# Cluster-masked attention and two MoE layers on one core: the first pair's cluster steps split by head, waits and priorities of the attention's planner set anew

## The chip, the core and the metric

The kernel runs on one core of a Trainium2 chip. A core has a matrix engine (PE, TensorE; its weight loads are listed as PEld), a vector engine (DVE, VectorE), a scalar engine (ACT, ScalarE), a general engine (POOL, GpSimd), and SP (SyncE), which issues the transfers. The metric is the device time of one execution in microseconds. A difference of less than 0.2% (1.2 us) is about what a measurement of this kernel cannot tell from no change.

## The reference

Two batches of eight heads, 768 tokens of 64 elements each, attend within clusters; the result goes through two layers.

```python
q_assign = np.argmax(np.einsum('bhsd,hcd->bhsc', q_n, c_n), axis=-1)
k_assign = np.argmax(np.einsum('bhsd,hcd->bhsc', k_n, c_n), axis=-1)
mask = q_assign[:, :, :, None] == k_assign[:, :, None, :]
scores = np.where(mask, scale * np.matmul(q, k.transpose(0, 1, 3, 2)), -1000000000.0)
scores = scores - np.max(scores, axis=-1, keepdims=True)
attn = np.exp(scores)
attn = attn / (np.sum(attn, axis=-1, keepdims=True) + 1e-09)
x = matmul(attn, v)                  # 1536 tokens x 512
h = x @ w_in                         # 512 x 2048
x = (h * sigmoid(1.702 * h)) @ w_out
# then a second layer: x @ w2_in, a softmax-weighted product, a norm, @ w2_out
```

There are 16 clusters; `q_n`, `k_n` and `c_n` are rows divided by their norms.

## The kernel before

**The attention.** There are 16 units u, one for each head and batch, taken in eight pairs p of two heads. For each pair the queries and keys are loaded (`load`), transposed on PE (`turn`, L557) into `ex`, split into a high and a low part (`turn_high` on ACT, `turn_low` L573 on DVE), and multiplied with the centroids. The products are copied and turned again, and then the cluster steps on DVE find each token's cluster: the maximum (`cluster_max`, L608), equality with it (L614), a weighting that picks the first of equals (L617), a maximum again (L623), and two comparisons that write the one-hot code `oh` (`cluster_halves`, L631, two instructions of half the size). The code of the first pair is turned on PE by `cluster_rows` (L647) and put in place by `cluster_place` (L655); `cluster_turn` (L639) turns the whole of it, and moves (L664, issued by SP) bring the rest into `OP`, the operands of the scores.

For each unit there are nine score tiles m of 512 columns, in two passes. The first pass, `sm` (`peak`, L936), computes scores with the clusters' codes appended; DVE takes the negative maximum of each token (`nma`, `peak_max`, L947), a small reduction makes `nm` of it (L959), PE turns that (L963), and it goes into the operands, for the first four units by `peak_rows` (L968) and for the others by a copy (L980) and a move. The second pass, `st` (`score`, L995 and L996), computes the scores less their maximum; ACT takes the exponential (L1004), ACT or DVE casts it to 16 bits (`cast`, L1009), POOL or DVE computes what the cast left off (`rest`, L1013), and PE multiplies both with the values (`av`, L1028, L1031, L1032). A further part on DVE and ACT normalizes the result (L1043 to L1058).

The values are scaled by powers of two that are worked out on DVE from 128x1 columns: `powers`, `factor` (L821, one product of two such columns) and `x_power` (L852 and L853, two products). POOL computes the low part of the values (`values_low`, L795 and L796).

**The layers.** `hps` (L1200) is the first product of the first layer; its weights are prepared on DVE during the attention (L196, L201, L205). The layers follow an order of their own, which starts where the attention's ends.

**What sets the order.** Every step is entered by `add` with the cost on each engine that may do it, a due time, the steps that it comes after, and the PSUM buffer that it takes or frees. `Plan.order` then simulates the engines: at each turn it takes, of the steps that are possible now, the one with the earliest due time, and the instructions are emitted in that order. Each engine works its own list strictly in order. A step marked `shared` on DVE is not placed beside a POOL step. SHIFTS is a table that adds to the due times of single steps, by their number. With STAY above zero, PE prefers for a while to stay with one kind of matmul. What a step waits for on the chip is set by the data that it touches, not by the planner's list.

Of the kernel before, what the change touches and what calls it, by code (L numbers as in the profile page):

```python
# [9 lines left out]
F32 = mybir.dt.float32  # L10
# [11 lines left out]
def kernel(  # L22
# [22 lines left out]
    P = 128  # L45
# [28 lines left out]
    XDUE = 30  # L74
    VDUE = 15
    VLC = dict(DVE=0.93, POOL=2.55)
    SOON = 10
# [18 lines left out]
    STAY = 0.0  # L96
# [71 lines left out]
    class Weight:  # L168
# [434 lines left out]
    def groups(t):  # L603
        return t.rearrange("p (g o) -> p g o", o=1).to_broadcast([P, G, C])

    def cluster_max(t, p):
        mxs[p] = oh_p.tile([P, G], F32, tag="mx", name="mx")
        nc.vector.tensor_reduce(out=mxs[p], in_=t["tile"], op=ALU.max, axis=AX.X)  # L608

    def cluster_equal(t, p):  # L610


        eqs[p] = t["tile"]
        nc.vector.tensor_tensor(out=eqs[p], in0=t["tile"], in1=groups(mxs[p]), op=ALU.is_equal)  # L614

    def cluster_weigh(p):
        nc.vector.tensor_tensor(  # L617
            out=eqs[p], in0=eqs[p], in1=first.rearrange("p (o c) -> p o c", o=1).to_broadcast([P, G, C]), op=ALU.mult
        )

    def cluster_first(p):
        m2s[p] = oh_p.tile([P, G], F32, tag="m2", name="m2")
        nc.vector.tensor_reduce(out=m2s[p], in_=eqs[p], op=ALU.max, axis=AX.X)  # L623

    def cluster_halves(p):

        eq = eqs.pop(p).rearrange("p (j s i) c -> p s j i c", s=2, i=2)
        m2 = m2s.pop(p).rearrange("p (j s i o) -> p s j i o", s=2, i=2, o=1)
        ohs[p] = oh_p.tile([P, NJ, 2, 2, C], BF16, tag="oh", name="oh")
        for s, op in enumerate((ALU.is_lt, ALU.is_equal)):  # L630
            nc.vector.tensor_tensor(  # L631
                out=ohs[p][:, :, s], in0=eq[:, s], in1=m2[:, s].to_broadcast([P, NJ, 2, C]), op=op
            )
# [54 lines left out]

    def operands_of(p):
# [4 lines left out]
        for s in range(2):  # L694
# [7 lines left out]
            for i in range(2):  # L702
                T["L", p, s, i] = add(
                    dict(SP=(0.65, 1.0)), n0 + LDUE if p > 1 else -62, lambda t, s=s, i=i: load(p, s, i),
                    after=[at("TT", p - 1, 2)] + late(True) if p > 1 else [],
                )
        for e in range(3):
# [4 lines left out]
                after=[a, at("ST", 2 * (p - NHL) + 1, NU - 1)],  # L712
# [5 lines left out]
        for n in range(2):  # L718
# [10 lines left out]
        b = add(dict(DVE=0.47), n0 + 18, lambda t, a=a: cluster_max(a, p), after=[a, at("C4", p - 1)])  # L729
        b = add(dict(DVE=0.47), n0 + 18, lambda t, a=a: cluster_equal(a, p), after=[b])  # L730
        b = add(dict(DVE=0.47), n0 + 19, lambda t: cluster_weigh(p), after=[b])
        b = add(dict(DVE=0.47), n0 + 20, lambda t: cluster_first(p), after=[b])
        b = T["C4", p] = add(
            dict(DVE=0.54), n0 + 21, lambda t: cluster_halves(p), after=[b, at("TO", p - 1)], frees=a
        )
        for e in range(0 if p else 3):
            a = add(dict(PE=0.3), n0 + 21, lambda t, e=e: cluster_rows(t, e), after=[b], take="ex")
# [4 lines left out]
        a = T["TO", p] = add(dict(PE=0.45), n0 + 22, lambda t: cluster_turn(t, p), after=[b], take="ex")  # L742
# [4 lines left out]
        for i in range(2):  # L747
            u = 2 * (p - NS) + i
            before = [at("ST", u, NU - 1), at("SM", u, NU - 1)]
# [58 lines left out]
    def values():  # L808
# [50 lines left out]
        add(dict(DVE=1.1), XDUE, lambda t, a=a: x_power(a), after=[a, scales["v"]], frees=a)  # L859
        T["VF"] = add(dict(DVE=0.1), 8, lambda t: factor(), after=list(scales.values()))  # L860
# [211 lines left out]
    def peaks_of(u):  # L1072
# [21 lines left out]
        if u >= RWS:  # L1094
# [9 lines left out]
            T["RW", u] = add(dict(SP=(0.65, 0.05)), n0 + NU - 18, lambda t: peak_row(u), after=[a, at("ST", u - 4, NU - 1)])  # L1104
# [3 lines left out]
    def scores_of(u):  # L1108
# [45 lines left out]
        if i:  # L1154
            a = add(
                dict(ACT=0.73, DVE=0.5), n + 12, lambda t: x_high(t, p), after=[T["N", u], T["N", u - 1], at("TX", p - 1, 0)],
# [150 lines left out]
    for p in range(NH // 2):  # L1307
# [743 lines left out]
```

## Time and profile before

| | |
|---|---|
| median of 3 runs | 592.21 us (592.07 to 593.05) |
| profiled execution | 592.09 us |
| its span in the trace | 590.3 us |
| PE busy | 579.9 us (98%) |
| DVE, ACT, POOL busy | 454.1, 418.5, 278.7 us |
| granted PE clock | 1.00 in every window |
| first matmul of hps | 219.65 us |

The span runs from the first to the last instruction that the trace holds; the execution's own time is 1.8 us longer. "Busy" of PE includes matmuls that overlap in its pipeline, so a busy PE can still be a little late.

### The profile page before, as it was taken

What the parts mean: (1) busy time and instruction counts of PE and PEld (TensorE: products, weight loads), DVE (VectorE), ACT (ScalarE), POOL (GpSimd) and SP (SyncE); (2) the same over time, 40 slices, a digit from 0 to 9 for tenths busy, and PEclk for the clock granted to TensorE, in tenths of its full rate; (3) what the DMA queues carried; (4) which work ended last, traced back from release to release, by engine and by line L of the source; (5) the groups of instructions that cost most, each with busy time, mean ns of one, the idle gap of its engine ahead of it and who ended that gap; (6) DMA issues with size and microseconds to landing.
All of it is one profiled execution on the core that took longest, in us unless ns stands there. A gap on an engine that the chain in (4) does not pass through costs nothing.

```text
span 590.3 us, 12602 instructions
## 1 busy us (share of the span) xinstructions
PE 579.9 (98%) x4790; PEld 387.1 (66%) x4790; DVE 454.1 (77%) x924; ACT 418.5 (71%) x799; POOL 278.7 (47%) x262
## 2 busy tenths in 40 slices
PE   7999999999999999999999999999999999999997
PEld 5788888888888876666666666666655664444444
DVE  5999998898999997899888731984996427996820
ACT  5799989988999978788878356563647614647831
POOL 7469979977778764344682037802100300133100
PEclk9999999999999999999999999999999999999999
DMA  8976969797773026443650530320000530043571
GB/s 206 229 190 151 218 136 204 154 193 154 152 146 63 17 64 203 146 140 145 213 180 1 179 109 0 108 72 0 1 2 1 72 72 0 37 72 82 113 146 53
DMA packets 79732, 65.28 MB, mean 111 GB/s; under 512 B 63620, under 2 KB 66520, under 8 KB 79672
## 3 DMA queue, kind: packets, MB, share of 16 engines
q1 hardware_dynamic: 79672, 64.49, 45.2%
q8 instruction: 37, 0.61, 0.4%
q14 instruction: 23, 0.19, 0.1%
HBM read 34.64 MB, written 3.15 MB: 64 GB/s over the span
## 4 chain that ended last, share of the span: by engine, by line
PE 92%; DVE 4%; ACT 1%; DMA 1%; issue 1%; SPq 0%; DVEq 0%; ACTq 0%
PE bank L1696 20%; PE hps L1200 16%; PE bank L1517 16%; PE st L995 6%; PE sm L936 5%; PE bank L1200 5%; PE bank L1551 5%; PE st L996 5%; PE av L1028 3%; PE av L1032 3%; PE ex L587 3%; PE av L1031 3%; PE ex L557 1%; DVE nma L947 1%; DMA reg<-in_q_dram 1%
## 5 line engine op out<-in xcount | busy, mean ns | idle before, releaser
L1013 POOL TENSOR_TENSOR ph<-p,ph 128x512 f16<-128x512 f32 x116 | 135.8, 1194 | 31.9 <-ACT ph L1009 17.8
L1200 PEld LDWEIGHTS <-reg 128*128 128x128 f16 x768 | 75.1, 98 | 48.9
L947 DVE TENSOR_REDUCE nma<-sm 128x1 f32<-128x512 f32 (+1 forms) x144 | 95.7, 681 | 5.7 <-PE sm L936 5.3
L1517 PE MATMUL bank<-g,reg 128*128 128x384 f16 x576 | 94.4, 326 | 0.0
L1200 PE MATMUL hps<-xT,reg 128*128 128x384 f16 x576 | 94.3, 326 | 0.0
L1517 PEld LDWEIGHTS <-reg 128*128 128x128 f16 x576 | 56.4, 98 | 37.2
L1215 POOL TENSOR_SCALAR g<-g,scl 128x384 f32<-128x384 f32 x40 | 37.4, 935 | 82.5 <-ACT g L1210 78.6
L1696 PE MATMUL bank<-reg,g 128*128 128x512 f16 (+1 forms) x366 | 75.0, 365 | 0.0
L1696 PEld LDWEIGHTS <-g 128*128 128x128 f16 x438 | 42.9, 98 | 46.8
L1004 ACT ACTIVATE p<-st 128x512 f32<-128x512 f32 x115 | 67.8, 601 | 7.8 <-PE st L996 5.0
L1009 ACT CAST ph<-p 128x512 f16<-128x512 f32 x107 | 64.2, 623 | 1.9 <-PE av L1032 1.2
L996 PE MATMUL st<-OP 97*128 97x512 f32 (+3 forms) x196 | 62.9, 336 | 0.0
L1028 PE MATMUL av<-vh,ph 128*128 128x65 f16 x576 | 62.2, 194 | 0.0
L1032 PE MATMUL av<-vh,ph 128*128 128x65 f16 x576 | 61.3, 195 | 0.7 <-DVE ph L1013 0.7
L1031 PE MATMUL av<-vh,ph 128*128 128x64 f16 x576 | 61.4, 193 | 0.0
L1028 PEld LDWEIGHTS <-ph 128*128 128x128 f16 x576 | 52.7, 99 | 11.0 <-issue 9.3
L936 PE MATMUL sm<-OP 80*128 80x512 f32 (+1 forms) x192 | 56.0, 359 | 1.7 <-DVE nma L947 1.4
L1032 PEld LDWEIGHTS <-ph 128*128 128x128 f16 x576 | 53.7, 97 | 1.0 <-DVE ph L1013 0.9
L1031 PEld LDWEIGHTS <-ph 128*128 128x128 f16 x576 | 53.8, 97 | 0.1
L1899 POOL TENSOR_TENSOR small<-small,mhalf 128x2 f32<-128x2 f32 (+1 forms) x7 | 4.6, 655 | 81.0 <-DVE small L1895 81.0
L1216 POOL TENSOR_TENSOR g<-g,g 128x384 f16<-128x384 f32 x40 | 40.4, 1010 | 3.3
L936 PEld LDWEIGHTS sm<-OP 80*128 80x128 f32 x192 | 33.8, 190 | 8.4 <-DVE nma L947 2.8
(255 smaller groups left out, 1188.3 us busy)
## 6 DMA issues: line engine op xcount, KB each, us to landing
OP<-hl SPq DMA_DIRECT2D x32, 384.0 KB, 5.3
raw<-in_moe_w_in_dram SPq DMA_DIRECT2D x24, 512.0 KB, 3.5
raw<-in_moe_w_out_dram SPq DMA_DIRECT2D x24, 512.0 KB, 4.2
xT<-in_v_dram SPq DMA_DIRECT2D x8, 384.0 KB
hl<-hl SPq DMA_DIRECT2D x8, 384.0 KB, 5.6
raw<-in_k_dram SPq DMA_DIRECT2D x12, 192.0 KB, 3.4
raw<-in_q_dram SPq DMA_DIRECT2D x12, 192.0 KB, 5.3
OP<-oht SPq DMA_DIRECT2D x30, 48.0 KB, 2.2
```

Of the source, the lines that this page charges most:

```text
L936: nc.tensor.matmul(t["tile"][:, at], Q1[0:KM, j * P:(j + 1) * P], K1[0:KM, cs], start=True, stop=True)
L947: nc.vector.tensor_reduce(out=out, in_=src, op=ALU.max, axis=AX.X, negate=True)
L996: nc.tensor.matmul(t["tile"][:, at], K1[0:n, ks], Q1[0:n, cs], start=False, stop=True)
L1004: nc.scalar.activation(p32s[u, m], t["tile"], AF.Exp, scale=SCALE)
L1009: e(phs[u, m][:, 0], p32s[u, m])
L1013: e.tensor_tensor(out=phs[u, m][:, 1], in0=p32s.pop((u, m)), in1=phs[u, m][:, 0], op=ALU.subtract)
L1028: nc.tensor.matmul(av[:, i, :], ph[:, 0, qs], vh[:, u, kt, D:], start=(m == 0 and kt == 0 and i == 0), stop=False,)
L1031: nc.tensor.matmul(av[:, i, 0:D], ph[:, 0, qs], vh[:, u, kt, 0:D], start=False, stop=False)
L1032: nc.tensor.matmul(av[:, i, :], ph[:, 1, qs], vh[:, u, kt, D:], start=False, stop=(m == NU - 1 and kt == NJ - 1 and i == NJ - 1),)
L1200: nc.tensor.matmul(self.ps, w1.at(c, m, e), xT[:, x, c, n * TB:(n + 1) * TB], start=(c == 0 and e == x), stop=(c == ND - 1 and e == 1),)
L1517: nc.tensor.matmul(out_, wo.at(f, c, e), lp["g", n][:, x, f, :], start=(f == 0 and e == x), stop=(f == NF - 1 and e == 1),)
L1696: nc.tensor.matmul(out_, data, weight, start=start and i == 0, stop=stop and i == n - 1)
```

## The change

The cluster steps take a head index i. For the first pair they are entered twice, once for each head, with half the elements in each instruction; for the other pairs i is None and they stay as they were. `cluster_rows` of the first pair now comes after the first head's code alone. Steps that used to be entered as coming after one tile of a unit are entered as coming after all nine (`all_of`), and some loads and moves get one more step to come after. `x_power` and `factor` are marked `shared`. Several constants change, and the whole SHIFTS table is replaced (98 entries by 82, of which a line each stands here).

```diff
-    XDUE = 30
+    XDUE = 90
-    SOON = 10
+    SOON = 6
-    STAY = 0.0
+    STAY = 2.0
...
+    def of_head(t, i):
+        if i is None:
+            return t
+        if len(t.shape) == 2:
+            return t.rearrange("p (g i) -> p i g", i=2)[:, i]
+        return t.rearrange("p (g i) c -> p i g c", i=2)[:, i]
...
-    def cluster_max(t, p):
-        mxs[p] = oh_p.tile([P, G], F32, tag="mx", name="mx")
-        nc.vector.tensor_reduce(out=mxs[p], in_=t["tile"], op=ALU.max, axis=AX.X)
+    def cluster_max(t, p, i):
+        if p not in mxs:
+            mxs[p] = oh_p.tile([P, G], F32, tag="mx", name="mx")
+        nc.vector.tensor_reduce(out=of_head(mxs[p], i), in_=of_head(t["tile"], i), op=ALU.max, axis=AX.X)
...
+    def all_of(name, u):
+        return [at(name, u, m) for m in range(NU)]
...
-                after=[a, at("ST", 2 * (p - NHL) + 1, NU - 1)],
+                after=[a] + all_of("ST", 2 * (p - NHL) + 1),
...
+        for i in (None,) if p else (0, 1):
+            c, d = (0.47, 0) if p else (0.28, i)
+            b = add(dict(DVE=c), n0 + d + 18, lambda t, y=y, i=i: cluster_max(y, p, i), after=[y, at("C4", p - 1)])
+            b = add(dict(DVE=c), n0 + d + 18, lambda t, y=y, i=i: cluster_equal(y, p, i), after=[b])
...
-            a = add(dict(PE=0.3), n0 + 21, lambda t, e=e: cluster_rows(t, e), after=[b], take="ex")
+            a = add(dict(PE=0.3), n0 + 21, lambda t, e=e: cluster_rows(t, e), after=[ones_of[0]], take="ex")
...
-            before = [at("ST", u, NU - 1), at("SM", u, NU - 1)]
+            before = all_of("ST", u) + all_of("SM", u)
...
-        add(dict(DVE=1.1), XDUE, lambda t, a=a: x_power(a), after=[a, scales["v"]], frees=a)
-        T["VF"] = add(dict(DVE=0.1), 8, lambda t: factor(), after=list(scales.values()))
+        add(dict(DVE=1.1), XDUE, lambda t, a=a: x_power(a), after=[a, scales["v"]], frees=a, shared=True)
+        T["VF"] = add(dict(DVE=0.1), 8, lambda t: factor(), after=list(scales.values()), shared=True)
...
-                    dict(SP=(1.25, 0.9)), n + 20, lambda t, e=e: x_turn(p, e),
+                    dict(SP=(1.5, 0.9)), n + 20, lambda t, e=e: x_turn(p, e),
...
-        38: -3, 65: -7, 119: 2.5, 144: -2.5, 146: 6.5, 200: -1, 208: -1.5, 227: -2, 233: 1, 265: 2, 270: -0.5,
+        12: 4, 36: -1, 67: 2, 107: 10.5, 130: 10, 137: -6, 144: -1, 149: 4, 204: 4, 282: -7.5, 307: -5.5, 314: 2,
```

In the changed file the lines of the attention stand some 20 to 29 numbers further down: L608 becomes L615, L631 becomes L648 and L650, L947 becomes L976, L1009 becomes L1038, L1013 becomes L1042, L821 becomes L850, L852 and L853 become L881 and L882.

**DVE, the first pair's cluster steps.** Before, from the low parts of the second pair (`hl`) on:

```order
L573 TENSOR_TENSOR hl<-ex,hl 128x512 x2
L608 TENSOR_REDUCE mx<-ex 128x24
L614 TENSOR_TENSOR ex<-ex,mx 128x384
L617 TENSOR_TENSOR ex<-ex,first 128x384
L623 TENSOR_REDUCE m_281<-ex 128x24
L631 TENSOR_TENSOR oh<-ex,m_281 128x6x32 x2
L573 TENSOR_TENSOR hl<-ex,hl 128x256 x2
L655 CAST OP_0_0_146<-ex 16x512
```

The same place in the changed kernel:

```order
L573 TENSOR_TENSOR hl<-ex,hl 128x256 x2
L573 TENSOR_TENSOR hl<-ex,hl 128x512
L615 TENSOR_REDUCE mx<-ex 128x12
L623 TENSOR_TENSOR ex<-ex,mx 128x12x16
L615 TENSOR_REDUCE mx<-ex 128x12
L629 TENSOR_TENSOR ex<-ex,first 128x12x16
L623 TENSOR_TENSOR ex<-ex,mx 128x12x16
L636 TENSOR_REDUCE m_284<-ex 128x12
L629 TENSOR_TENSOR ex<-ex,first 128x12x16
L650 TENSOR_TENSOR oh<-ex,m_284 128x6x16 x2
L636 TENSOR_REDUCE m_284<-ex 128x12
L650 TENSOR_TENSOR oh<-ex,m_284 128x6x16 x2
```

The six instructions are twelve of half the size, the two heads alternate, and the second pair's two small low parts stand ahead of them instead of behind.

**DVE, the products of 128x1 columns.** Before, `x_power` (L852, L853) between the score maxima of the sixth unit:

```order
L617 TENSOR_TENSOR ex<-ex,first 128x384
L947 TENSOR_REDUCE nma<-sm 128x1
L147 TENSOR_REDUCE scl<-ex 128x1
L149 TENSOR_SCALAR scl<-scl 128x1
L150 TENSOR_SCALAR scl<-scl 128x1
L151 TENSOR_SCALAR scl<-scl 128x1
L155 TENSOR_SCALAR scl<-scl 128x1 x2
L852 TENSOR_TENSOR scl<-scl 128x1
L853 TENSOR_TENSOR scl<-scl 128x1
L947 TENSOR_REDUCE nma<-sm 128x2
L623 TENSOR_REDUCE m_1438<-ex 128x24
L947 TENSOR_REDUCE nma<-sm 128x1
```

In the changed kernel `factor` (L850) stands between maxima of the fifth unit (before, it stood right behind the powers that it comes from, ahead of the cluster steps of pair p=2 and among the maxima of the third unit):

```order
L976 TENSOR_REDUCE nma<-sm 128x1 x3
L976 TENSOR_REDUCE nma<-sm 128x2
L976 TENSOR_REDUCE nma<-sm 128x1
L988 TENSOR_REDUCE nm<-nma 128x6
L1072 TENSOR_SCALAR ri<-av 128x6
L850 TENSOR_TENSOR scl<-scl 128x1
L976 TENSOR_REDUCE nma<-sm 128x2
```

and `x_power` (L881, L882) stands past the maxima of the twelfth unit:

```order
L881 TENSOR_TENSOR scl<-scl 128x1
L882 TENSOR_TENSOR scl<-scl 128x1
L988 TENSOR_REDUCE nm<-nma 128x6
L1038 CAST ph<-p_3242 128x512
L205 SCALAR_TENSOR_TENSOR reg_105<-raw,reg_105 128x512
L1009 CAST mr<-ex 6x128
L573 TENSOR_TENSOR hl<-ex,hl 128x256 x2
L1042 TENSOR_TENSOR ph<-st,ph 128x512
L1072 TENSOR_SCALAR ri<-av 128x6
L1074 RECIPROCAL ri<-ri 128x6
L1080 TENSOR_TENSOR xs<-av,ri 128x6x64
L976 TENSOR_REDUCE nma<-sm 128x1 x2
```

`x_power` has moved from the sixth to the twelfth unit, where nine rows of other work lie between it and the next score maxima; `factor` has moved later, to where the next row is a score maximum.

**DVE, the end of the attention.** Before:

```order
L1013 TENSOR_TENSOR ph<-st,ph 128x512
L1009 CAST ph<-st 128x512
L205 SCALAR_TENSOR_TENSOR reg_105<-raw,reg_105 128x512
L1013 TENSOR_TENSOR ph<-st,ph 128x512
L1009 CAST ph<-st 128x512
L196 TENSOR_SCALAR reg_105<-raw 128x512
L1013 TENSOR_TENSOR ph<-st,ph 128x512
L201 SCALAR_TENSOR_TENSOR reg_105<-raw,reg_105 128x512
```

After:

```order
L1038 CAST ph<-st 128x512
L1042 TENSOR_TENSOR ph<-st,ph 128x512
L1038 CAST ph<-st 128x512
L201 SCALAR_TENSOR_TENSOR reg_105<-raw,reg_105 128x512
L1042 TENSOR_TENSOR ph<-st,ph 128x512 x2
L205 SCALAR_TENSOR_TENSOR reg_105<-raw,reg_105 128x512
L196 TENSOR_SCALAR reg_105<-raw 128x512
L201 SCALAR_TENSOR_TENSOR reg_105<-raw,reg_105 128x512
L205 SCALAR_TENSOR_TENSOR reg_105<-raw,reg_105 128x512
```

The last exponential's cast has moved from DVE to ACT, and between the last two rests, where a cast and a step of the weights (L196) stood, there is nothing now. On PE, the first twelve matmuls of `hps` now stand ahead of the last twelve of `av`; before, they stood behind them.

## Rows read from the trace of the kernel before

**Rows 1.** Windows: us, then busy us (instructions) of each engine, clock, DMA share, GB/s.

```profile
40.00:50.00 10.00, 9.56 (x105) 7.97 (x104) 9.42 (x23) 9.90 (x19) 9.55 (x9) 1.00 0.91 192
60.00:70.00 10.00, 10.00 (x146) 8.56 (x142) 9.83 (x23) 9.46 (x20) 9.04 (x8) 1.00 0.92 199
70.00:80.00 10.00, 9.04 (x110) 7.60 (x106) 9.58 (x24) 7.71 (x16) 7.45 (x7) 1.00 0.70 175
80.00:150.00 70.00, 70.00 (x905) 60.40 (x904) 62.31 (x124) 63.91 (x123) 60.93 (x52) 1.00 0.85 172
150.00:200.00 50.00, 49.71 (x678) 42.65 (x675) 46.91 (x97) 47.34 (x91) 40.58 (x35) 1.00 0.51 104
220.00:550.00 330.00, 330.00 (x1921) 187.80 (x1920) 244.02 (x458) 206.64 (x402) 102.72 (x102) 1.00 0.29 83
```

**Rows 2.** Waits of PE: engine, line, releaser: us in total, times, longest.

```profile
PE sm L936 <- DVE nma L947: 1.4, 2, 1.0
PE av L1032 <- DVE ph L1013: 0.7, 2, 0.5
PE st L995 <- DVE nma L947: 0.6, 1, 0.6
```

**Rows 3.** Timeline of DVE, first pair's cluster steps: start us, duration us, instruction.

```profile
13.81 0.55 DVE L608 TENSOR_REDUCE mx<-ex 128x24 f32<-128x384 f32 x1
14.39 0.57 DVE L614 TENSOR_TENSOR ex<-ex,mx 128x384 f32<-128x384 f32 x1
16.19 0.62 DVE L631 TENSOR_TENSOR oh<-ex,m 128x192 bf16<-128x192 f32 x2
```

**Rows 4.** Timeline of DVE, a later pair's half-size steps and what follows.

```profile
75.42 0.61 DVE L631 TENSOR_TENSOR oh<-ex,m 128x192 bf16<-128x192 f32 x2
75.95 0.68 DVE L947 TENSOR_REDUCE nma<-sm 128x1 f32<-128x512 f32 x1
```

**Rows 5.** Timeline of DVE, the wait for the first row of maxima.

```profile
22.06 0.42 DVE L968 TENSOR_TENSOR OP<-tx,ident 6x256 fp32r<-6x256 f32 x1 [0.50 <-PE tx L963]
```

**Rows 6.** Timeline of DVE, the factor of the values and the narrow step ahead.

```profile
40.12 0.15 DVE L151 TENSOR_SCALAR scl<-scl 128x1 uint32<-128x1 uint32 x1
40.50 1.05 DVE L821 TENSOR_TENSOR scl<-scl 128x1 f32<-128x1 f32 x1
```

**Rows 7.** Timelines of DVE, POOL and PE around 73 us.

```profile
71.75 0.96 DVE L852 TENSOR_TENSOR scl<-scl 128x1 f32<-128x1 f32 x1
72.64 1.20 DVE L853 TENSOR_TENSOR scl<-scl 128x1 f32<-128x1 f32 x1
73.76 0.68 DVE L947 TENSOR_REDUCE nma<-sm 128x2 f32<-128x512 f32 x1
...
69.30 5.63 POOL L1013 TENSOR_TENSOR ph<-p,ph 128x512 f16<-128x512 f32 x5
...
72.91 0.28 PE L995 MATMUL st<-hl 128*128 128x256 f32 x1
73.14 0.39 PE L936 MATMUL sm<-OP 80*128 80x512 f32 x1
74.50 0.50 PE L936 MATMUL sm<-OP 80*128 80x256 f32 x2 [0.96 <-DVE nma L947]
```

**Rows 8.** Timelines of DVE and PE at the end of the attention.

```profile
218.58 0.69 DVE L1013 TENSOR_TENSOR ph<-st,ph 128x512 f16<-128x512 f32 x1
...
217.45 0.19 PE L1031 MATMUL av<-vh,ph 128*128 128x64 f16 x1
217.79 0.20 PE L1032 MATMUL av<-vh,ph 128*128 128x65 f16 x1 [0.15 <-DVE ph L1013]
...
218.57 0.19 PE L1028 MATMUL av<-vh,ph 128*128 128x65 f16 x1
218.60 0.19 PE L1031 MATMUL av<-vh,ph 128*128 128x64 f16 x1
219.32 0.20 PE L1032 MATMUL av<-vh,ph 128*128 128x65 f16 x1 [0.53 <-DVE ph L1013]
```

More of the change, by code (lines that the diff above doesn't have):

```diff
@@ L613, in cluster_equal @@
+    def cluster_max(t, p, i):
+        if p not in mxs:
+            mxs[p] = oh_p.tile([P, G], F32, tag="mx", name="mx")
+        nc.vector.tensor_reduce(out=of_head(mxs[p], i), in_=of_head(t["tile"], i), op=ALU.max, axis=AX.X)
+    def cluster_equal(t, p, i):
         eqs[p] = t["tile"]
-        nc.vector.tensor_tensor(out=eqs[p], in0=t["tile"], in1=groups(mxs[p]), op=ALU.is_equal)
-    def cluster_weigh(p):
+        x, m = of_head(t["tile"], i), of_head(mxs[p], i)
+        n = m.shape[1]
         nc.vector.tensor_tensor(
-            out=eqs[p], in0=eqs[p], in1=first.rearrange("p (o c) -> p o c", o=1).to_broadcast([P, G, C]), op=ALU.mult
+            out=x, in0=x, in1=m.rearrange("p (g o) -> p g o", o=1).to_broadcast([P, n, C]), op=ALU.is_equal
@@ L619, in cluster_weigh @@
         )
[L621 to L629, printed above, removed]
-        for s, op in enumerate((ALU.is_lt, ALU.is_equal)):
-            nc.vector.tensor_tensor(
-                out=ohs[p][:, :, s], in0=eq[:, s], in1=m2[:, s].to_broadcast([P, NJ, 2, C]), op=op
-            )
+    def cluster_weigh(p, i):
+        x = of_head(eqs[p], i)
+        nc.vector.tensor_tensor(
+            out=x, in0=x, in1=first.rearrange("p (o c) -> p o c", o=1).to_broadcast([P, x.shape[1], C]), op=ALU.mult
+        )
@@ new lines, in cluster_first, with cluster_halves @@
+    def cluster_first(p, i):
+        if p not in m2s:
+            m2s[p] = oh_p.tile([P, G], F32, tag="m2", name="m2")
+        nc.vector.tensor_reduce(out=of_head(m2s[p], i), in_=of_head(eqs[p], i), op=ALU.max, axis=AX.X)
+    def cluster_halves(p, i):
+        eq = eqs[p].rearrange("p (j s i) c -> p s i j c", s=2, i=2)
+        m2 = m2s[p].rearrange("p (j s i o) -> p s i j o", s=2, i=2, o=1)
+        if p not in ohs:
+            ohs[p] = oh_p.tile([P, NJ, 2, 2, C], BF16, tag="oh", name="oh")
+        oh = ohs[p].rearrange("p j s i c -> p s i j c")
+        for s, op in enumerate((ALU.is_lt, ALU.is_equal)):
+            if i is None:
+                o, x, m = (y.rearrange("p i j c -> p j i c") for y in (oh[:, s], eq[:, s], m2[:, s]))
+                nc.vector.tensor_tensor(out=o, in0=x, in1=m.to_broadcast([P, NJ, 2, C]), op=op)
+            else:
+                nc.vector.tensor_tensor(
+                    out=oh[:, s, i], in0=eq[:, s, i], in1=m2[:, s, i].to_broadcast([P, NJ, C]), op=op
+                )
@@ L704, in operands_of @@
                     dict(SP=(0.65, 1.0)), n0 + LDUE if p > 1 else -62, lambda t, s=s, i=i: load(p, s, i),
-                    after=[at("TT", p - 1, 2)] + late(True) if p > 1 else [],
+                    after=[at("TT", p - 1, s), at("TT", p - 1, 2)] + late(True) if p > 1 else [],
                 )
@@ L741, in operands_of @@
             )
-        a = T["TO", p] = add(dict(PE=0.45), n0 + 22, lambda t: cluster_turn(t, p), after=[b], take="ex")
+        a = T["TO", p] = add(dict(PE=0.45), n0 + 22, lambda t: cluster_turn(t, p), after=ones_of, take="ex")
         b = add(
@@ L1103, in peaks_of @@
             )
-            T["RW", u] = add(dict(SP=(0.65, 0.05)), n0 + NU - 18, lambda t: peak_row(u), after=[a, at("ST", u - 4, NU - 1)])
+            T["RW", u] = add(dict(SP=(0.65, 0.05)), n0 + NU - 18, lambda t: peak_row(u), after=[a] + all_of("ST", u - 4))
     todo, held = [], []
@@ L1155, in scores_of @@
             a = add(
-                dict(ACT=0.73, DVE=0.5), n + 12, lambda t: x_high(t, p), after=[T["N", u], T["N", u - 1], at("TX", p - 1, 0)],
+                dict(ACT=0.73, DVE=0.5), n + 12, lambda t: x_high(t, p), after=[T["N", u], T["N", u - 1], at("TX", p - 1, 0), at("TX", p - 1, 1)],
                 tail=True, shared=True,
```

20 lines of the change are left out of this document (10 added, 10 removed), and 16 rows, old and new, of the table SHIFTS.

## The prediction

> **What bounds the kernel now.** The table by windows is read first. From 220 us on PE loses nothing for 330 us, and between 80 and 150 us nothing either [rows 1]. The layers' steps are not touched by the change and start when the attention's last matmul has run, so whatever the change does has to happen ahead of 219.65 us, where the first product of the layers starts, and is then handed on unchanged. Ahead of that point PE is the bound too, with a few holes: 0.44 us between 40 and 50 us, 0.96 us between 70 and 80 us, 0.29 us between 150 and 200 us [rows 1]. The waits of PE say who makes them: VectorE, with the score maxima (1.4 and 0.6 us) and with the last rests of the exponentials (0.7 us) [rows 2]. All that can be won is therefore a few us of 592; what can be lost has no such limit.
>
> The timelines show three holes closely. Around 73 us, `x_power`'s two products of 128x1 columns take 0.96 and 1.20 us, although a narrow step on the same kind of column takes 0.15 us [rows 6, 7]. GpSimd meanwhile runs five rests from 69.30 us on, 5.63 us in all, 1.126 us each, so that one ends at 72.68 and the next at 73.81 us; L852 ends at 72.71 and L853 at 73.84 us [rows 7]. VectorE is held until a rest ends, twice. The maximum behind it starts at 73.76 us, and the `sm` matmul that waits for it at 74.50 us, 1.36 us behind the one ahead, where two matmuls of half its size take 0.23 us (72.91 to 73.14 us) [rows 7]. Net: 1.36 - 0.23 = 1.13 us. At the end of the attention, two groups of `av` wait for rests: 0.34 and 0.72 us from start to start where neighbours start 0.03 us apart, so 0.31 + 0.69 = 1.0 us [rows 8]. The third is early: VectorE waits 0.50 us for the turn of the first maxima, ahead of 22.06 us [rows 5].
>
> **The change, part by part.** The sum is made against the profiled execution, 592.09 us, which is 0.12 us below the median of the runs shown.
>
> *The first pair's cluster steps: +0.2 us.* Before, they run from 13.81 to 16.19 + 0.62 = 16.81 us, 3.0 us, at 0.58 us from one step to the next, which needs it [rows 3]. Two steps of half size that don't need each other take 75.95 - 75.42 = 0.53 us, 0.265 each [rows 4]. A half-size step that needs the one ahead is not in the trace: at least 0.265, at most 0.58 us; halving the elements takes off at most 0.265 us, so at least 0.32 us; I take 0.39 us. The order of the changed kernel puts eq of head 0, mx of head 1, weigh of head 0 and so on in turn, and each of these still has a wait for the step right ahead of it, since the two heads' strided views of one tile overlap. Seven such starts lie ahead of the first head's two comparisons: 7 x 0.39 + 2 x 0.265 = 3.3 us, 0.3 us more than both heads took. The rows of the first head's code go on from there. Against that, the second pair's small low parts no longer stand behind the steps. I take +0.2 us; the bounds are -0.1 (at 0.32 us a step, and the low parts' place won) and +0.4 us.
>
> *18 to 52 us: -0.55 us.* The changed order puts one more score maximum ahead of the first row of maxima, into the idle 0.50 us [rows 5], so that VectorE is that much further on in a stretch in which PE waits for it: 0.6 us at L995 and 0.44 us between 40 and 50 us [rows 1, 2]. `factor`, held for 1.05 us at 40.50 us [rows 6], leaves this stretch as well. Together up to 1.04 us is to be had. On the other side `sm` matmuls now stand further ahead, and there PE can wait for maxima where it did not. I take half; the bounds are -1.0 and +0.3 us.
>
> *`factor`, later: +0.5 us.* Its next row is now a score maximum, among the maxima of the fifth unit (around 62 us before). There VectorE is busy for 9.83 of 10 us and GpSimd for 9.04 [rows 1], so a hold moves on to PE in full. It is between nothing and one rest of 1.126 us [rows 7], on average half.
>
> *`x_power` out of the sixth unit: -1.13 us*, the hole above. Of this the whole goes, since the `sm` behind had no other late releaser.
>
> *`x_power` in the twelfth unit: +0.3 us.* Nine rows of casts, rests and low parts lie between it and the next score maximum, and GpSimd is busy for 40.58 of 50 us between 150 and 200 us [rows 1], so two holds are likely again, but PE has fewer steps to wait for behind them: the turn of `nm` and the rest. The bounds are 0 and the 1.13 us that it cost at its old place. The Trainium skill, "SBUF — State Buffer", section "Who interferes with whom", says that a VectorE instruction with two SBUF inputs contends with a GpSimd instruction that reads SBUF, and that whichever issues first holds the port for its whole instruction; the trace agrees (ends at 72.71 and 73.84 against 72.68 and 73.81 us). By that rule alone the move removes nothing, since GpSimd works on at the new place, and the sum would be some 0.8 us higher; it is the first rival.
>
> *GpSimd's order: +0.2 us.* Of the values' low parts, one that stood behind 35 rests now stands behind 30, and one that stood behind 47 stands behind 53. Five rests, around 75 to 85 us, are therefore later by one such part. It has two instructions of 768 elements, and a rest has 512: from the rest's 1.126 us an estimate is 2.3 (no dependence on size) to 3.4 us. GpSimd is idle for 2.55 of 10 us there [rows 1], which covers most of it. The bounds are 0 and 1.0 us.
>
> *The end of the attention: -1.0 us.* The last cast leaves VectorE, which had the last rest at 218.58 us and PE at 219.32 us [rows 8], and no step stands between the last two rests. Twelve matmuls of the layers, of 384 columns, now run ahead of the last `av`: by the 0.115 us for 256 columns, 0.17 us each, an estimate of 2.1 us, twice the wait to be covered. The other bound is +0.3 us, if ACT's cast comes late.
>
> All the rest, the declared waits, the loads' new order, STAY and the transfers' price, I cost at nothing: the same matmuls run (five idle fillers less), and what the order changes is hidden under PE, which is full between 80 and 150 us. If that cover is gone, it shows as a new wait there.
>
> The sum: 0.2 - 0.55 + 0.5 - 1.13 + 0.3 + 0.2 - 1.0 = -1.48, so 592.09 - 1.48 = **590.6 us**, 1.6 us or 0.27% below the median.
>
> **The rivals.** *The holds only move.* Speaking for it: VectorE is held by GpSimd wherever GpSimd is busy, and it is busy at both new places. `factor` then costs a whole rest (1.13 instead of 0.5 us) and `x_power` its 1.13 us again (instead of 0.3): -1.48 + 0.63 + 0.83 = 0.0, so 592.1 us. Against it: behind `x_power` stands no score maximum now.
>
> *Late rests, slower.* If the five rests that have moved behind a low part of the values find `av` already waiting, PE stands for the whole part, up to 3.4 us: -1.48 - 0.2 + 3.4 = +1.7, so 593.8 us. It decides from a wait of 2.9 us on (593.4 us, 0.2% above the median). Against it speaks GpSimd's 2.55 us of idle time there; for it, that it was busy for 9.04 of the 10 us ahead [rows 1].
>
> *More is won.* If VectorE's early lead keeps and none of the three smaller losses comes: 0.2 - 1.0 - 1.13 - 1.0 = -2.9, so 589.2 us. Against it: `factor` must land in a gap of a GpSimd that is 90% busy.
>
> **How the numbers follow.** The forecast's case has 0.50, with its own range from 589.6 to 591.6 us; 0.42 of it lie below 591.0 us. That the holds only move has 0.21, late rests 0.15, more won 0.14. Faster by over 0.2% (1.2 us, about what a measurement of this kernel can tell from no change) is 0.42 + 0.14 = 0.56; within 0.2% 0.08 + 0.21 = 0.29; slower 0.15. The range, 588.8 to 593.2 us, takes in the second and the last rival and leaves out most of the late rests.
>
> **What would show it.** Right: the first `sm` of the changed kernel 0 to 0.4 us later; no wait of PE for a maximum around 73 us; a VectorE product of some 1 us (L850) around 62 us with a wait of PE behind it; no `av` waiting at the end; the first product of the layers at about 218.2 us and the same 370.7 us from there to the end of the span. Wrong: a new wait of PE over 1 us between 75 and 212 us, most of all at `av` around 80 us for a rest by GpSimd, or behind L881 and L882; or a start that is over 0.5 us later, which would show that half-size steps cost nearly what whole ones do.

## The result: 1.2% slower

| | before | changed |
|---|---|---|
| median of 5 runs each, side by side | 592.21 us (591.45 to 593.44) | 599.81 us (597.44 to 600.8) |
| profiled execution | 592.09 us | 597.44 us |
| its span | 590.3 us | 595.4 us |
| first matmul of `hps` | 219.65 us | 220.99 us |
| from there to the end of the span | 370.7 us | 374.4 us |

The ratio of the medians is 1.0123, 95% interval 1.0107 to 1.0139: 7.6 us slower, where 1.6 us faster was forecast, and far outside the range. The profiled execution is the fastest of the changed kernel's five, so its trace shows 5.35 of the 7.6 us. It shows them in two places: 1.34 us up to the first `hps`, and 3.7 us behind it, where the prediction held that nothing could change. The last twelve `av` now run behind the first twelve `hps`, from 222.94 to 223.31 us, so 0.37 of the 3.7 us still belong to the attention: 1.7 us are lost there and 3.4 us in the layers.

One window of the kernel before, and then the windows of the changed kernel (columns as in [rows 1]):

```profile
30.00:40.00 10.00, 10.00 (x146) 8.62 (x146) 9.63 (x25) 10.00 (x22) 5.73 (x5) 1.00 0.76 199
...
30.00:40.00 10.00, 9.32 (x103) 7.63 (x102) 8.87 (x21) 10.00 (x22) 7.34 (x7) 1.00 0.76 198
40.00:50.00 10.00, 10.00 (x149) 8.76 (x147) 9.57 (x25) 9.69 (x19) 9.32 (x9) 1.00 0.96 202
60.00:70.00 10.00, 9.40 (x111) 7.79 (x110) 10.00 (x20) 8.44 (x16) 8.77 (x8) 1.00 0.82 188
70.00:80.00 10.00, 9.23 (x125) 7.72 (x124) 9.49 (x21) 8.57 (x17) 8.88 (x8) 1.00 0.70 159
80.00:150.00 70.00, 69.41 (x894) 59.10 (x893) 65.68 (x125) 63.67 (x123) 58.28 (x48) 1.00 0.85 170
220.00:550.00 330.00, 327.13 (x1934) 186.70 (x1933) 245.17 (x455) 204.92 (x400) 103.69 (x102) 1.00 0.29 83
```

Beside these and [rows 1], PE has lost 2.87 us in the layers (330.00 to 327.13), 0.68 us between 30 and 40 us, 0.60 us between 60 and 70 us and 0.59 us between 80 and 150 us, four windows in which it had lost nothing. The hole between 40 and 50 us is gone (10.00 against 9.56 us); the one between 70 and 80 us is still there: 9.23 against 9.04 us. PE's waits in the changed kernel (columns as in [rows 2]):

```profile
PE bank L1578 <- ACT reg L239: 1.3, 1, 1.3
PE ex L557 <- DVE nma L976: 1.0, 2, 0.6
PE st L1024 <- DVE ph L1042: 0.8, 1, 0.8
PE bank L1578 <- ACT g L1236: 0.7, 1, 0.7
PE ex L666 <- DVE oh L650: 0.7, 1, 0.7
PE st L1024 <- ACT p L1033: 0.6, 1, 0.6
PE sm L965 <- DVE nma L976: 0.5, 2, 0.4
PE hps L1229 <- DVE g L1247: 0.4, 1, 0.4
PE bank L1578 <- DVE reg L242: 0.3, 1, 0.3
...
PE av L1061 <- DVE ph L1042: 0.2, 1, 0.2
```

The two long waits that were to go have gone: `sm` for a maximum fell from 1.4 to 0.5 us, `av` at the end from 0.7 to 0.2 us. In their place stand the four waits of the first layer (three of `bank`, the second product, and one of `hps`), two turns (L557), two score tiles (L1024; one waits for a rest, the other for an exponential), and the turn of the first head's code (L666), which waited 0.2 us before.

Around 70 us the timelines of DVE, POOL and PE, one after the other, show what fills the old hole:

```profile
68.44 1.69 DVE L1038 CAST ph<-p 128x512 f16<-128x512 f32 x1
70.51 0.68 DVE L1042 TENSOR_TENSOR ph<-st,ph 128x512 f16<-128x512 f32 x1
...
68.19 1.65 POOL L1091 TENSOR_TENSOR xh<-xs,xh 128x768 f16<-128x768 f32 x1
...
71.24 0.39 PE L1024 MATMUL st<-hl 128*128 128x256 f32 x1 [0.77 <-DVE ph L1042]
```

A cast (L1038) starts on VectorE 0.25 us after a GpSimd instruction of 1.65 us, takes 1.69 us and ends 0.29 us behind that instruction's end. The same cast takes 0.42 us at 160.39 us (below), where no GpSimd instruction runs as it starts. The rest L1042 behind it on VectorE's list comes late, and PE stands 0.77 us for it, the whole of what it loses between 70 and 80 us. It looks like the hold of `x_power` [rows 7], on another instruction. `x_power` itself is not held at its new place (by line: durations in ns, least, median and most, and the starts):

```profile
L881 DVE TENSOR_TENSOR scl<-scl x1: 159/159/159, 160.2 to 160.2; 128x1 f32<-128x1 f32 x1
L882 DVE TENSOR_TENSOR scl<-scl x1: 151/151/151, 160.2 to 160.2; 128x1 f32<-128x1 f32 x1
```

The timelines of DVE and POOL there show why:

```profile
160.39 0.42 DVE L1038 CAST ph<-p 128x512 f16<-128x512 f32 x1
...
157.93 1.16 POOL L1042 TENSOR_TENSOR ph<-p,ph 128x512 f16<-128x512 f32 x1 [0.21 <-POOL ph L1042]
160.88 1.54 POOL L1042 TENSOR_TENSOR ph<-p,ph 128x512 f16<-128x512 f32 x1 [1.79 <-DVE ph L1038]
```

GpSimd stands idle from 159.09 to 160.88 us, and both products fall into this gap.

In the layer, the timelines of DVE (the first five rows), ACT (two) and PE (three):

```profile
284.54 1.28 DVE L205 SCALAR_TENSOR_TENSOR reg<-raw,reg 128x512 uint32<-128x512 uint32 x2
288.18 0.62 DVE L1247 SCALAR_TENSOR_TENSOR g<-hps,scl,g 128x384 f16<-128x384 f32 x1 [1.49 <-ACT g L1239]
288.71 0.68 DVE L201 SCALAR_TENSOR_TENSOR reg<-raw,reg 128x512 uint32<-128x512 uint32 x1
312.33 0.62 DVE L1247 SCALAR_TENSOR_TENSOR g<-hps,scl,g 128x384 f16<-128x384 f32 x1 [3.44 <-ACT g L1239]
312.87 0.17 DVE L147 TENSOR_REDUCE scl<-tot 128x1 f32<-128x16 f32 x1
...
285.25 0.63 ACT L218 ACTIVATE junk<-reg 128x512 bf16<-128x512 f32 x1 [1.72 <-DVE reg L205]
287.56 0.58 ACT L1239 ACTIVATE g<-hps,scl 128x384 f16<-128x384 f32 x1
...
302.31 7.96 PE L1229 MATMUL hps<-xT,reg 128*128 128x384 f16 x48 [0.42 <-DVE g L1247]
310.10 0.29 PE L141 MATMUL tot<-wss,ones 128*128 128x16 f32 x2
317.57 0.50 PE L1578 MATMUL bank<-g,reg 128*128 128x384 f16 x2 [1.32 <-ACT reg L239]
```

Two engines wait for each other. ACT stands 1.72 us for a weight of `w_out` (L205 on VectorE), with gates (L1239) listed behind its square (L218). VectorE then stands 1.49 us for one of these gates, with the next weights (L201) listed behind its low part (L1247). At the end of the weights PE sums the squares (`tot`, L141) at 310.10 us, but VectorE makes the power from it (L147) only at 312.87 us, behind one more low part that waits 3.44 us for its gate. Before, 0.66 us lay between the two (DVE, then PE):

```profile
308.46 0.17 DVE L147 TENSOR_REDUCE scl<-tot 128x1 f32<-128x16 f32 x1
...
307.80 0.29 PE L141 MATMUL tot<-wss,ones 128*128 128x16 f32 x2
313.79 4.39 PE L1551 MATMUL bank<-g,reg 128*128 128x384 f16 x26
```

The second product then comes 2.4 us later, counted from the first `hps` (96.6 us, where it was 94.15 us); 0.37 us of this are the twelve `av`.

### The profile page after: what moved, and what is told of

It reads as the page before. It is cut to its first block, busy times and chain, and to the rows that moved or that the text cites. A ratio compares the mean times of both kernels' runs of the same rounds, so it can differ in the third digit from the quotient of the medians.

```text
span 595.4 us, 12613 instructions
## 1 busy us (share of the span) xinstructions
PE 582.2 (98%) x4785; PEld 387.0 (65%) x4785; DVE 459.7 (77%) x932; ACT 419.5 (70%) x798; POOL 280.6 (47%) x261
## 4 chain that ended last, share of the span: by engine, by line
PE 72%; DVE 17%; ACT 5%; DMA 4%; issue 2%; POOL 0%; SPq 0%; DVEq 0%; ACTq 0%; POOLq 0%
PE bank L1723 20%; PE bank L1544 16%; PE bank L1229 5%; PE st L1024 5%; PE bank L1578 5%; PE st L1025 5%; PE sm L965 4%; DVE reg L201 3%; DVE reg L205 3%; PE av L1057 3%; PE av L1061 2%; PE av L1060 2%; DVE nma L976 2%; PE ex L587 2%; DVE reg L242 2%
## 5 line engine op out<-in xcount | busy, mean ns | idle before, releaser
L1042 POOL TENSOR_TENSOR ph<-p,ph 128x512 f16<-128x512 f32 x116 | 137.9, 1209 | 36.0 <-ACT ph L1038 15.8
L976 DVE TENSOR_REDUCE nma<-sm 128x1 f32<-128x512 f32 (+1 forms) x144 | 94.8, 680 | 6.4 <-PE sm L965 5.7
L1038 ACT CAST ph<-p 128x512 f16<-128x512 f32 x109 | 65.3, 624 | 1.8 <-PE av L1061 1.1
```

The source lines that it names most:

```text
L976: nc.vector.tensor_reduce(out=out, in_=src, op=ALU.max, axis=AX.X, negate=True)
L1038: e(phs[u, m][:, 0], p32s[u, m])
L1042: e.tensor_tensor(out=phs[u, m][:, 1], in0=p32s.pop((u, m)), in1=phs[u, m][:, 0], op=ALU.subtract)
```

## The experiments

In most of these kernels the planner's order is written out as a list of steps, each with its engine, and then edited or joined from the two kernels' lists. So the code is that of one kernel, and only the sequence on the engines changes. All compute the whole reference. Each median stands against runs of the kernel before on the same chip.

**Where the loss is: attention or layer.**

```diff
-LISTED = changed
+LISTED = attention(changed) + layer(before)    (e2)
+LISTED = attention(before) + layer(changed)    (e3)
```

> The attention's steps in the order of the changed kernel, the first layer's own steps (its weights, products, gates) in the order of the kernel before; the lists are written out and the code is that of the change. Theory A, that the first layer's new order costs what the attention does not: the waits of PE between 300 and 320 us (3.4 us in the profile) go, what is left is the attention's own loss of 1.7 us, and the median is 593 to 595. Rival B, that the layer is late because the attention hands over fewer prepared weights: the waits stay and the median is 597 or more.

Measured: 594.90 us (594.49 to 595.02), before 591.98; ratio 1.0048 (1.0035 to 1.0061). From the first `hps` to the end its trace has 370.6 us, as before the change.

> The mirror image: the attention's steps in the order of the kernel before, the first layer's own steps in that of the changed kernel. Theory A: 592.2 plus the 3.4 us of the profile, up to plus the 5.9 us by which the median of the change exceeds the attention's 1.7 us: 595.6 to 598.1. Rival B: within 1 us of 592.2.

Measured: 597.46 us (595.96 to 599.07), ratio 1.0093 (1.0076 to 1.0111); 375.7 us from the first `hps` to the end. So the attention's order costs 2.9 us and the layer's 4.7 to 5.5 us (7.6 - 2.9, or 597.46 - 591.98). The layer's order, which the prediction left out, is the larger part.

**Where in the layer.** First, the power alone, moved ahead of the low part that it stood behind:

```diff
-1806 (low part, L1247), 1626 (power, L147)
+1626 (power), 1806 (low part)
```

> The changed kernel with one step moved on VectorE's list: the power of w_out (narrow 128x1 steps that the high and low parts of w_out need) stands ahead of the low part of a gelu block (L1247) instead of behind it; every other list is unchanged. In the profile of the changed kernel that power starts at 312.87 us although PE's total for it ran at 310.10 us, because the low part ahead waits 3.44 us for ScalarE. Theory A, that this position passes the delay on to PE: the power starts about 2.4 us earlier, the first high part (316.80 us) about 2.3 us earlier, PE's waits of 1.3 and 0.3 us at the second product go, and the median falls from 599.8 by 1.5 to 2.5 us to 597.3 to 598.3. Rival B, that VectorE's whole list is late there and something else ends last: within 0.5 us of 599.8.

Measured: 597.82 us (597.3 to 598.08), ratio 1.0099 (1.0086 to 1.0112). The median is 2.0 us lower, but the fastest runs are the same (597.3 and 597.44), and so is the stretch from the first `hps` to the end (374.3 us). Its waits in the layer have only changed their names:

```profile
PE hps L1234 <- DVE g L1252: 1.5, 2, 1.2
PE bank L1676 <- ACT g L1241: 1.2, 1, 1.2
```

So the power's place is not the cause by itself; that it makes some runs longer is what four runs beside five suggest, and no more. Next, the lists of one engine alone:

```diff
-layer(changed)
+layer(changed), VectorE's steps in the sequence of before    (e13)
+layer(changed), ScalarE's steps in the sequence of before    (e14)
```

> Edit: the changed kernel, but VectorE's steps of the layer in the order of before (98% of them in that sequence; ScalarE's 88% and TensorE's all in the order of the change). With the whole layer's order of before it was 594.9, with the changed one 599.8. Theory V (the loss comes from VectorE's order: one w_out step more behind the first layer matmul, the powers behind a low part): 595 to 596.5. Rival S (ScalarE's order, with the high parts ahead of the gates, is what the tensor engine waits for): 598.5 to 600.

> Edit: the changed kernel, but ScalarE's steps of the layer in the order of before (97% of them in that sequence; VectorE's 93% and TensorE's all in the order of the change). Theory V (VectorE's order makes the loss): 598.5 to 600. Rival S (ScalarE's order makes it): 595 to 596.5. Both at 597 to 598: the loss is shared.

Measured: 599.52 us (598.36 to 600.1) and 607.19 us (605.06 to 607.93). The first lies where rival S put it, but the second, which should then have been fast, is 7.4 us slower still. The lists of the two engines fit only each other, and a mixed pair makes waits of its own (`hps` for a gate, 1.7 us at once in both). These runs part nothing. Cutting by time leaves each engine's list fitting the other's:

```diff
-layer(changed)
+layer(changed) up to 236 us of the plan, then layer(before)    (e16)
+layer(before) up to 236 us, then layer(changed)                (e17)
+layer(changed) up to 285 us, then layer(before)                (e18)
```

> Edit: the changed kernel, with the layer's steps in its own order up to 236 us of the plan (which holds the end of attention and the first w_out weights) and in the order of before behind that. Theory H (the loss is made in the handover, where VectorE starts w_out's weights some 2 us later against the first layer matmul): 598 to 600. Rival L (it is made by the order from there to 320 us, the high parts, gates, low parts and the power): 594.5 to 596.

> Edit: the reverse: the layer's steps in the order of before up to 236 us of the plan, and in the changed kernel's behind that. Theory H: 594.5 to 596. Rival L: 598 to 600. Where both are near 597, the loss is shared.

Measured: e16 594.42 us (593.96 to 595.98), e17 598.98 us (598.16 to 599.18), before 591.83. The handover at the end of the attention costs nothing; my theory H fell, and the rival holds. With the later order of before, e16's PE loses 0.17 us in the layers and VectorE's two low parts run together behind their gates, without a wait:

```profile
220.00:550.00 330.00, 329.83 (x1953) 188.28 (x1950) 248.09 (x460) 207.26 (x403) 104.21 (x102) 1.00 0.29 85
...
290.71 1.13 DVE L1252 SCALAR_TENSOR_TENSOR g<-hps,scl,g 128x384 f16<-128x384 f32 x2
```

> Edit: the changed kernel, with the layer's steps in its own order up to 285 us of the plan and in the order of before behind that. Of the layer's 316 us mark only the last 30 us are then of before: the last w_out weights, gates, low parts, squares and the power. Theory E (the loss is made by the order of these last steps): 594.3 to 595.5, as with the cut at 236 us. Rival M (it is built up between 236 and 285 us, where VectorE falls behind with w_out's weights): 597.5 to 599.5.

Measured: 598.80 us (598.5 to 599.71), before 591.89. Rival M's number holds: with the last 30 us as before the loss is all there. Its timelines, DVE and then PE:

```profile
289.88 0.62 DVE L1252 SCALAR_TENSOR_TENSOR g<-hps,scl,g 128x384 f16<-128x384 f32 x1 [1.50 <-ACT g L1244]
300.17 0.62 DVE L1252 SCALAR_TENSOR_TENSOR g<-hps,scl,g 128x384 f16<-128x384 f32 x1 [2.48 <-ACT g L1244]
...
312.65 0.40 PE L141 MATMUL tot<-wss,ones 128*128 128x16 f32 x2 [2.04 <-ACT junk L218]
```

VectorE's wait of 1.5 us for a gate is the same as in the changed kernel; that of 2.48 us may come from the seam of the two lists. So may PE's of 2.04 us for `tot`, which the changed kernel does not have: what part of e18's loss the seam makes is not known. The wait of 1.5 us stands in the traces of all five kernels that lose 3.6 us or more from the first `hps` to the end (the changed one, e1, e3, e17, e18), and in none of before, e2, e7 and e16, which lose at most 0.6 us there (in e7 and e16 0.4 of it by the twelve `av`; e13 and e14, with mixed lists, are left out). No run took it out alone, so that it is the cause is argued and not shown. M's reason, that VectorE falls behind with the weights, isn't shown either: its last weight of `w_out` (L205) ends 87.4 us after the first `hps` in the changed kernel and 87.6 us after it in e7, which has no such loss. PE's own sequence in the layer is another in the changed kernel too; e16 to e18 cut all engines' lists together, and no run changes PE's alone.

**Where in the attention.** The list of before, with one thing changed in each:

```diff
 attention(before)
+cluster steps split by head, in their old place                 (e4)
+changed order up to 17 us of the plan                           (e9)
+changed order up to 40 us                                       (e10)
+split in the old place, and the changed order from 40 us on     (e15)
```

> The kernel before with only the first pair's cluster steps split by head and alternating on VectorE, as the change has them; all other lists are those of before (four idle fillers on PE less). My step says +0.2 us (-0.1 to +0.4): 592.4. Rival: the split is what makes the start late and costs a few us: over 593.5.

Measured: 593.15 us (592.31 to 594.4), ratio 1.0025 (1.0016 to 1.0034), so +1.2 us, between the two. DVE's timeline:

```profile
13.91 0.35 DVE L620 TENSOR_REDUCE mx<-ex 128x12 f32<-128x192 f32 x1
14.30 0.37 DVE L628 TENSOR_TENSOR ex<-ex,mx 128x192 f32<-128x192 f32 x1
17.40 0.42 DVE L655 TENSOR_TENSOR oh<-ex,m 128x96 bf16<-128x96 f32 x2
17.74 0.75 DVE L578 TENSOR_TENSOR hl<-ex,hl 128x256 fp32r<-128x256 f32 x2
18.52 0.69 DVE L679 CAST OP<-ex 16x512 fp32r<-16x512 f32 x1
```

A half step that waits for the one ahead starts 0.39 us after it, as the prediction had it. The whole lasts until 17.82 us, 1.0 us later than in [rows 3], and the placing (L679) comes only behind the low parts, at 18.52 us.

> Edit: the kernel before, but its first 17 us (in the planner's times) in the order of the changed kernel: the cluster steps split by heads, Q's load ahead of K's, and the small low parts ahead of the steps; behind that everything stands as before. Split alone cost 1.2 us. Theory A (the loads and low parts ahead win back what the split costs; the start is not where the changed kernel's attention loses): 591.4 to 592.4, first score matmul at about 18.2 us. Rival (the split is a good part of the attention's loss of 2.9): 592.8 or more.

> Edit: as the start to 17 us, but the changed kernel's order up to 40 us of the plan, so that the second pair's ranking stands where the change has it (its turns and reductions between the maxima of the first scores), and the order of before behind it. Theory A (the losses between 25 and 33 us, where the tensor engine waits for a bank's maximum, are a good part of the attention's 2.9): 0.8 to 1.8 over the start to 17 us, so 592.5 to 594. Rival (what is late there is caught up in the next 10 us, and the loss comes later): within 0.4 of the start to 17 us.

Measured: e9 591.98 us (590.72 to 593.69), e10 593.85 us (593.22 to 595.07), before 592.16. With the loads and low parts that the change also moves, the split costs nothing; the stretch from 17 to 40 us costs 1.9 us. The windows of e9 and then of e10:

```profile
30.00:40.00 10.00, 10.00 (x138) 8.51 (x135) 9.41 (x25) 10.00 (x22) 5.74 (x5) 1.00 0.76 201
...
30.00:40.00 10.00, 9.32 (x106) 7.66 (x105) 8.84 (x21) 10.00 (x23) 7.42 (x7) 1.00 0.81 200
```

PE loses 0.68 us between 30 and 40 us in e10, as in the changed kernel, and nothing in e9. The first `hps` comes at 219.40 us in e9 and at 220.75 us in e10.

> Edit: the order of before up to 40 us of the plan (with the cluster steps split in their old place), the changed kernel's from there to the end of attention, and the layer of before. The whole attention of the change was 2.9 slower than before, its order up to 40 us with the rest of before 1.7 slower, and the split alone 1.2 slower. Theory A (the two halves add up): the part from 40 us is worth +1.2 beside before's start, and with the split in its old place +2.0 to +2.6: 594.1 to 594.8. Rival (the part behind 40 us loses only because the part ahead of it came late): 593.4 or less, the split's price alone or better.

Measured: 594.06 us (593.87 to 594.29), before 591.96: 0.9 us over the split alone. The parts add up: -0.2 (e9) + 1.9 + 0.9 = 2.6 us, beside e2's 2.9. So the part from 40 us on loses, although it holds `x_power` and the end of the attention, which are each a gain (below). Its trace has new waits of this kind; no run took them out, so that they make the loss is argued:

```profile
PE st L1029 <- DVE ph L1047: 0.7, 1, 0.7
PE ex L562 <- DVE nma L981: 0.5, 1, 0.5
```

**Single steps of the attention.** Two at their new place in the order of before, alone and together (e5, e6, e7), and two put elsewhere in e2's order (e8, e11):

```diff
 order(before)
+x_power behind the twelfth unit's maxima                                 (e5)
+last cast on ACT, no weights between the last rests, 12 hps ahead of av  (e6)
+both                                                                     (e7)
+both, and the changed order up to 17 us without the split                (e12)
 attention(changed) + layer(before)
+factor at its old place                                                  (e8)
+the third pair's second turn, L562, some entries later on PE             (e11)
```

In e11 one step of ScalarE also stands one place later.

> The kernel before with one step moved: the total for x_power on PE and x_power's seven rows on VectorE stand behind the maxima of the twelfth unit, as in the changed kernel, instead of among those of the sixth. My step: the hold of 2.1 us on VectorE and PE's wait of 1.13 us around 73 us go and the new place costs PE 0 to 0.3 us: 592.0 falls by 0.8 to 1.1 to 590.9 to 591.2. Rival, that the holds only move: within 0.3 of 592.0.

Measured: 590.52 us (589.66 to 592.17), ratio 0.9978 (0.9969 to 0.9988); first `hps` at 218.20 us. PE has 9.86 us between 70 and 80 us, where it had 9.04 [rows 1]. Here too the products fall into a gap of GpSimd: they start at 157.03 and 157.11 us, and GpSimd is idle from 156.51 to 159.47 us.

> The kernel before with the end of the attention as the change has it: the last cast on ScalarE, nothing between VectorE's last two rests (two steps of the weights stand behind them), and the first twelve matmuls of the layer ahead of the last twelve of av. My step: PE's waits for the last rests (1.0 us) go: 591.0. Rival, that VectorE's chain of weight steps decides the second product of the layer at 314 us: the 1.0 us comes back there as a wait of PE, and the median is within 0.3 of 592.0.

Measured: 591.02 us (590.12 to 592.95), ratio 0.9987 (0.9979 to 0.9995).

> Both of these edits together on the kernel before. My steps add up: 592.0 - 1.1 - 1.0 = 589.9. Rival, VectorE's weight steps: in the trace of before the first high part of w_out is there some 1.7 us ahead of the second product that needs it, so a gain beyond 1.7 us comes back as a wait at 314 us and the median is 590.3 or more.

Measured: 590.16 us (589.31 to 592.22), ratio 0.9975 (0.9966 to 0.9985); before 591.94 for e5 to e8. The two gains, 1.4 and 0.9 us, would make 2.3 us; the 1.8 us measured (by the interval 0.9 to 2.0 us) can't settle whether they add up.

> The kernel with the attention of the change and the layer of before (594.9 us), with one row of VectorE moved: factor stands where it stood before, right behind the powers it comes from, instead of among the maxima of the fifth unit. In the profile of the change it is held there for 1.04 us and PE waits 0.56 and 0.48 us behind it. If those waits are its doing: 593.9 to 594.2. Rival, that VectorE is late there anyway or is held as long at the earlier place: within 0.4 of 594.9.

Measured: 595.03 us (594.38 to 596.86), as e2. At its old place `factor` takes 0.16 us at 41.47 us and is not held (GpSimd is idle from 41.15 to 41.72 us), and PE is busy 0.42 us longer between 58 and 75 us than in e2's trace. Against that stands a wait of 0.86 us for an exponential at 26 us, ahead of either place of `factor`. The two lists are the same up to there, so the move did not make this wait; e8 can't settle what `factor`'s place is worth.

> Edit: the attention of the changed kernel with the layer of before (594.9), and in it the third pair's second turn on the tensor engine (L562 here) four entries later, so that it no longer stands for 0.75 us at 31.4 us for a maximum of the bank that it writes. Theory A (that wait is a loss of its own): 0.5 to 1.0 less, 593.9 to 594.4. Rival (the tensor engine then waits at its next score for the same maxima, since VectorE sets the pace there): 594.6 to 595.2.

Measured: 596.32 us (595.39 to 597.32), 1.4 us slower than e2, worse than either expectation. PE's waits from 24 to 40 us in e2 (first row) and in e11:

```profile
PE ex L562 <- DVE nma L981: 0.6, 1, 0.6
...
PE sm L970 <- DVE nma L981: 0.6, 1, 0.6
```

The turn's wait has become the next score tile's wait for the same maxima: VectorE sets the pace there. e11 has two more waits in this stretch, 0.6 us for an exponential and 0.2 us for `nm`. Why the time rises by 1.4 us on top was not settled.

> Edit: the kernel before with x_power later and the end of attention of the changed kernel (590.16 before), and the changed kernel's start up to 17 us of the plan with the cluster steps left whole. Theory A (Q's load and the low parts ahead are worth 0.2 to 0.6 where the split doesn't spend it): 589.4 to 590.0. Rival (they are worth nothing): 590.1 to 590.5.

Measured: 589.63 us (589.2 to 591.35), ratio 0.9962 (0.9951 to 0.9974), before 592.16. This version is faster than both kernels.

## Why the prediction was wrong

**The step that failed** is the premise "The layers' steps are not touched by the change and start when the attention's last matmul has run, so whatever the change does has to happen ahead of 219.65 us … and is then handed on unchanged." The section on the kernel before says that the layers follow an order of their own. Up to the second product of the first layer that is not so: its weights, products and gates are steps of the same planner, entered just ahead of the SHIFTS table, and the table moves their due times too (of the new one: 1478, 1480, 1496, 1621 and ten more). Nor does the layer start when the attention has ended, since twelve `hps` stand ahead of the last `av`. I read the order only at the three places in the attention that I had terms for, and took [rows 1], PE full from 220 us on, as proof that nothing could be lost there. A PE without a hole says that the present order is good enough, and nothing of another order. e2 and e3 put 4.7 to 5.5 of the 7.6 us on this, and e16 and e17 put it behind 236 us of the plan (e18 adds ahead of 285 us, if its seam costs nothing). Which wait there makes it stays open.

**The terms of the sum.**
- *Cluster steps, +0.2 us.* The 0.39 us for a dependent half step was exact (0.39 us, 13.91 to 14.30), but taken between 0.32 and 0.58 us without a reason, so that is luck. Alone the split costs 1.2 us; with the loads and low parts moved ahead it costs nothing (e9, -0.2 us with an interval from -0.6 to +0.5). The term was right for the change as a whole.
- *18 to 52 us, -0.55 us.* Wrong in sign: +1.9 us between 17 and 40 us (e10 less e9). Of the gain, the 0.44 us between 40 and 50 us came. But I wrote that `sm` matmuls "now stand further ahead, and there PE can wait for maxima where it did not", and bounded that by +0.3 us; it outweighed the gain. The longest wait for maxima in that stretch is a turn's (L557, 0.6 us), not an `sm`'s.
- *`factor`, +0.5 us.* It is held for 1.04 us, and PE waits 0.40 us behind it. What putting it back is worth, e8 can't say.

The changed kernel's timelines for it, DVE and PE:

```profile
61.58 1.04 DVE L850 TENSOR_TENSOR scl<-scl 128x1 f32<-128x1 f32 x1
62.54 0.68 DVE L976 TENSOR_REDUCE nma<-sm 128x2 f32<-128x512 f32 x1
...
63.28 0.50 PE L965 MATMUL sm<-OP 80*128 80x512 f32 x1 [0.40 <-DVE nma L976]
```

- *`x_power`, -1.13 and +0.3 us.* The gain is right, -1.4 us alone (e5), but not the account of the new place: I took two holds there as likely, from GpSimd's busy time over 50 us. The products take 0.159 and 0.151 us, since GpSimd is idle for 1.79 us just then. The rival that the holds only move fell for this instruction on its premise, that GpSimd is busy at the new place, and not on the rule of the hold. The change marks both steps `shared`, which keeps them apart from GpSimd in the plan; I left that out of the account. On the chip it held for `x_power` and not for `factor`. In the changed kernel a cast's hold at 68.44 us takes the place of the gain.
- *The end of the attention, -1.0 us.* Right: -0.9 us alone (e6); 0.2 us of the waits are left.
- *GpSimd's order, +0.2 us.* No `av` waits for GpSimd between 75 and 212 us; the rival of late rests did not come about. (By its own sum it would have decided from a wait of 3.0 us on, not 2.9.)
- *All the rest at nothing.* Wrong beside the layer too: PE loses 0.59 us between 80 and 150 us, where I counted on its being full as cover.

Of the signs that the prediction named, the missing wait for a maximum around 73 us and L850 came as written, and the `av` at the end nearly so. The first `sm` did not: it came 0.2 us earlier than before (18.16 us), where 0 to 0.4 us later was written. Nor did the first `hps` (220.99, not 218.2 us) and the stretch behind it (374.4, not 370.7 us). None of the three rivals had the mechanism. The one on the slower side put the loss in a single late rest; it came as many small waits and from the layer.

## What to carry to other kernels

A table of due times reaches every step that shares the planner. Before terms are costed, compare the order over the whole span and find the last row that differs; here that was some 90 us behind the point from which I took everything as unchanged. A bound engine that shows no hole has slack of unknown size in its suppliers, and a reordering can spend it. Take the good parts singly: two moves of this change, with its start, give 589.63 us, while the whole change costs 7.6 us.

## What the runs showed of the hardware that was not expected

VectorE's products of 128x1 columns take 0.15 to 0.16 us or about 1 us by whether a GpSimd instruction is running when they start: L881 and L882 were not held although GpSimd is busy for 40.65 of the 50 us around them, since they fell into a gap of 1.79 us. `factor` took 0.16 us in a gap of 0.57 us in e8, and 1.05 us in the kernel before [rows 6], where a rest runs on GpSimd from 40.37 us on. The busy share of a stretch does not tell whether one instruction in it is held. A cast of 128x512 with a single input took 1.69 us beside a GpSimd instruction of 1.65 us, and 0.42 us elsewhere. The Trainium skill, "SBUF — State Buffer", section "Who interferes with whom", says that a cast too can take the port pair that VectorE shares with GpSimd, and that the one that issues first has it for its whole instruction; the trace agrees here (GpSimd from 68.19 to 69.84 us, the cast until 70.13 us).
